# Weight conversions with a scale in place of a maximum and a mask, and a later product for the global tokens

## The chip, the cores and the metric

The kernel runs on one core of a Trainium2 chip. The metric is the time of one execution in microseconds (us) on the device, as the median of several runs. The engines are TensorE (PE in the profile, its weight loads PEld), VectorE (DVE), ScalarE (ACT), GpSimd (POOL) and SyncE (SP), which issues nearly all DMAs. Each engine works through its own queue in order. The profile gives the clock that TensorE is granted as a share of 2.4 GHz; there are two levels, 1.2 and 2.4 GHz.

## What is computed

Three layers in a row. The weights of the second and third layer arrive as 64-bit floats; the rest is 32-bit.

```python
# 1: attention, 4 batches x 8 heads, 512 local tokens (window of 32 to each side) and 32 global tokens, head size 64
a_l = sm([q_l k_g^T, where(mask, q_l k_l^T, -1e9)] / 8);  out_l = a_l @ [v_g, v_l]
out_g = sm(q_g [k_g, k_l]^T / 8) @ [v_g, v_l]
x = out.transpose(0, 2, 1, 3).reshape(2176, 512)      # 2048 local and 128 global tokens
# 2: gated layer, 512 -> 1536 -> 512
gate = 1 / (1 + exp(-(x @ w_gate)));  val = x @ w_val
x = (gate * val) @ w_out
# 3: rational layer, 512 -> 2048 -> 512
h = x @ w_in
P = a0 + a1*h + a2*h**2 + a3*h**3
Q = 1 + |b0|*|h| + |b1|*h**2
out = (P / (Q + 1e-6)) @ w_out
```

## The kernel before

**Number format.** Every operand of a matmul in layers 2 and 3 is split into a high part, rounded to the matmul's format, and a low part, the rest. A product is three matmuls: high by high, high by low, low by high. So each weight must be converted from 64 bits to 32, then split. `Weights` does that in blocks of 128x512, 68 in all: 24 `gv` (gate and value, two to each of the 12 feature blocks of layer 2), 12 `out` of layer 2, and 16 `in` and 16 `out` of layer 3 (the rational blocks). The steps of one block `j`, in the order of `Weights.order`:

- `fetch`: DMA of 512 KB into one of three `raw` buffers, issued by `bits` of three blocks before.
- `magnitude` (L565, L566): two ScalarE instructions, the absolute value of the upper words read as a 32-bit float into `v`, and the lower words scaled by 2^-29 into `q`.
- `bits` (L573 to L575): three VectorE instructions, a maximum with a tiny constant, a shift with a mask, and the OR with the top two bits of the upper word. Then the next fetch.
- `add` (L582): GpSimd adds `q`.
- `hi` (L604): ScalarE casts the high part. `lo` (L612): GpSimd subtracts it for the low part, and DMAs write the result to memory (`keep`); it is loaded again when the ring of twelve weight places has room.
- For the `gv` blocks of the features from 2 on also `sums` (L629 to L632), which forms the four weight sums of Strassen's scheme from two blocks, with VectorE, GpSimd, VectorE, VectorE in a row, and `splits` (L641, L642), two casts and two subtractions.

**Stages.** The attention runs first, to about 125 us, by a list of steps with due times (`STEPS`), into which the first conversions are woven. Then `gated` for layer 2: the tokens stand in five tiles, four of 512 and one (`GLOB`, the 128 global tokens). A first loop, called passes 0 to 5 here, runs over pairs of feature blocks `f0`, `f0 + 1` and treats tiles 0 and 1 and the global tile. In a pass TensorE's order is: first product (gate, then value) of `f0` with tile 0; the two halves of the second product for tile 1 of the pass before; first product of `f0 + 1` with tile 0; the global first product (L721 to L723); first product of `f0` with tile 1; the two halves of the second product for tile 0; two transposes of the global tile (`turn`, L788); first product of `f0 + 1` with tile 1; and the global second product (`second_glob`, L796 to L798). Behind each first product ScalarE takes the sigmoid (L750), VectorE multiplies (L751), ScalarE casts the high part (L758) and VectorE subtracts for the low part (L763). The sums of the second products are added on VectorE (L844, L805 for the global tile).

Between these stands `spot`, which lets `Pace` issue as many of the conversion steps of this pass as its share of 34 us allows; what is left is issued at the end of the pass. So the place of each conversion step in the queues of ScalarE, VectorE and GpSimd is fixed by the program's order. `AT_ONCE` says how many rational blocks are converted in each pass beside the six of the gated layer (pass 5: rational ones alone).

Then tiles 2 and 3: the first two feature blocks plainly, the other ten with Strassen's scheme (`strassen`), seven products in place of eight, with the rest of the conversions spread by another `Pace` over 132 us. From about 585 us on `rational` runs layer 3.

**PSUM.** First products take their banks in turn from a pool of three (`ps1`), second products, `turn` and `second_glob` from a pool of five (`ps2`). A pass takes nine banks of the first pool: two for each of four first products and one for the global one.

Of the kernel before, what the change touches and what calls it, by code (L numbers as in the profile page):

```python
# [8 lines left out]
F32 = mybir.dt.float32  # L9
F32R = mybir.dt.float32r  # L10
U32 = mybir.dt.uint32
AF = mybir.ActivationFunctionType
ALU = mybir.AluOpType
# [11 lines left out]
DM, FF, FF2 = 512, 1536, 2048  # L25
NTOK = B * (S + SG)
BIG = -8.0e9
F64_TINY = 2.0**-15
G1, G2 = 2, 4
Q_CONST = 1.0 + 1e-6  # L30
LN_SCALE = 2.0**-32
# [418 lines left out]
class Weights:  # L450
# [4 lines left out]


    EARLY, AHEAD = 4, 3
    AT_ONCE = (0, 2, 2, 2, 2, 5)
    RING2 = (4, 5, 6, 7, 0, 1, 2, 3, 8, 9, 10, 11)

    def __init__(self, tc, early, dram, ins, outs):
# [14 lines left out]
        for p, f in enumerate(range(2, NF + 1, 2)):  # L476
            m = n + self.AT_ONCE[p]
            if f < NF:
# [76 lines left out]
    def magnitude(self, j):  # L555

        key = self.order[j]
        name = "".join(map(str, key))
        r = self.staged[j]
        if self.combined(key):  # L560
            v = self.only.tile([128, 512], U32, tag="z", name=f"v{name}", bufs=5)
        else:
            v = self.early.tile([128, 512], U32, tag="v", name=f"v{name}", bufs=3)
        q = self.early.tile([128, 512], U32, tag="q", name=f"q{name}", bufs=3)
        self.nc.scalar.activation(v.bitcast(F32), r[:, :, 1].bitcast(F32), AF.Abs)  # L565
        self.nc.scalar.activation(q, r[:, :, 0], AF.Copy, scale=2.0**-29)  # L566
        self.staged[j] = r[:, :, 1], v, q

    def bits(self, j):

        high, v, q = self.staged[j]
        nc = self.nc
        nc.vector.tensor_scalar_max(v.bitcast(F32), v.bitcast(F32), F64_TINY)  # L573
        nc.vector.tensor_scalar(v, v, 3, 0x3FFFFFF8, ALU.logical_shift_left, ALU.bitwise_and)
        nc.vector.scalar_tensor_tensor(v, high, 0xC0000000, v, ALU.bitwise_and, ALU.bitwise_or)  # L575
        if j >= self.EARLY:
            self.fetch(j + self.AHEAD)

# [45 lines left out]
    def sums(self, j):  # L624

        nc, f = self.nc, self.order[j][1]
        v0, v1 = (self.whole[1, f, "gv", k] for k in range(2))
        g0, a0, g1, a1 = v0[:, 0:256], v0[:, 256:512], v1[:, 0:256], v1[:, 256:512]
        nc.vector.tensor_tensor(a1, a0, a1, ALU.add)  # L629
        nc.gpsimd.tensor_tensor(a0, g0, a0, ALU.subtract)  # L630
        nc.vector.tensor_tensor(g0, a1, g0, ALU.subtract)
        nc.vector.tensor_tensor(g1, g1, g0, ALU.subtract)  # L632

# [74 lines left out]
def layer(nc, ps, wp, net, f, i, mh, ml):  # L708

    for k in range(4):  # L710
        wh, wl = wp.block(net, f, i, k)
        nc.tensor.matmul(ps, wh, mh[:, k], start=k == 0, stop=False)  # L712
        nc.tensor.matmul(ps, wh, ml[:, k], start=False, stop=False)  # L713
        nc.tensor.matmul(ps, wl, mh[:, k], start=False, stop=k == 3)  # L714
# [20 lines left out]
def gated(nc, pools, only, xpool, dram, wp, ident, xh, xl):  # L735
# [7 lines left out]
    def new_acc(i):  # L743
        n = TILES[i][1]
        acc[i] = pools.acc.tile([128, 4, n], F32, tag=f"acc{i if i == GLOB else i % 2}", name=f"gacc{i}")

    def gate(pg, pv, name):

        t = pools.t.tile([128, 512], F32, tag="u", name=f"t{name}")[:, 0 : pg.shape[1]]
        nc.scalar.activation(t, pg, AF.Sigmoid)  # L750
        nc.vector.tensor_tensor(t, pv, t, ALU.mult)  # L751
        return t
# [12 lines left out]
    def split(t, name):  # L765
        g = high(t, name)
        low(t, g)
        return g

    def first(f, i):  # L770
        pg = pools.ps1.tile([128, 512], F32, tag="p1", name=f"pg{f}_{i}")
        pv = pools.ps1.tile([128, 512], F32, tag="p1", name=f"pv{f}_{i}")
        layer(nc, pg, wp, 1, f, "gate", xh[i], xl[i])
        layer(nc, pv, wp, 1, f, "val", xh[i], xl[i])
        return split(gate(pg, pv, f"{f}_{i}"), f"{f}_{i}")
# [8 lines left out]
    def turn(f0, t):  # L784

        ps = pools.ps2.tile([128, 512], F32, tag="p2", name=f"pt{f0}")
        for g in range(G):
            nc.tensor.transpose(ps[:, g * 128 : g * 128 + 128], t[:, g * 128 : g * 128 + 128], ident)  # L788
        gh, gl = split(ps[:, 0 : G * 128], f"{f0}_glob")
        return [(gh[:, g * 128 : g * 128 + 128], gl[:, g * 128 : g * 128 + 128]) for g in range(G)]  # L790

    def second_glob(f0, gs):
        ps = pools.ps2.tile([128, 512], F32, tag="p2", name=f"p2{f0}_glob")
        for k, (gh, gl) in enumerate(gs):
            wh, wl = wp.outer(1, f0 + k)
            nc.tensor.matmul(ps, gh, wh, start=k == 0, stop=False)  # L796
            nc.tensor.matmul(ps, gh, wl, start=False, stop=False)
            nc.tensor.matmul(ps, gl, wh, start=False, stop=k == G - 1)  # L798
        if f0 == 0:
            new_acc(GLOB)  # L800
        a = acc[GLOB].rearrange("p m t -> p (m t)")
        if f0 == 0:
            nc.vector.tensor_copy(a, ps)
        else:
            nc.vector.tensor_tensor(a, ps, a, ALU.add)  # L805

    def final_glob():

        n = TILES[GLOB][1]
        ps = pools.ps1.tile([128, 512], F32, tag="p1", name="pty")  # L810
        for m in range(4):
            nc.tensor.transpose(ps[:, m * n : m * n + n], acc[GLOB][:, m], ident)
        yh[GLOB] = xpool.tile([128, 4, n], F32R, tag=f"xh{GLOB}", name=f"yh{GLOB}")
        yl[GLOB] = xpool.tile([128, 4, n], F32R, tag=f"xl{GLOB}", name=f"yl{GLOB}")
        src = ps.rearrange("p (m t) -> p m t", m=4)
        nc.scalar.copy(yh[GLOB], src)
        nc.vector.tensor_tensor(yl[GLOB], src, yh[GLOB].bitcast(F32), ALU.subtract)
# [42 lines left out]
    def pair_of(f0, i, gs):  # L860
        return [lambda h=h: second(f0, i, gs, h) for h in range(2)]
# [7 lines left out]
    def ztile(name):  # L869
        return only.tile([128, 512], F32, tag="z", name=name, bufs=5)  # L870
# [11 lines left out]
    def less(dst, x, y, eng):  # L882

        for d, a, b in zip(dst, x, y):
            eng.tensor_tensor(d, a, b, ALU.subtract)
        eng.tensor_tensor(dst[0], dst[0], dst[1], ALU.add)

    def at(rc, k):
        return [t[:, k] for t in part[rc]]

    def c1(k):
        held["a", k], held["b", k] = ztile(f"za{k}"), ztile(f"zb{k}")
        less((held["a", k], held["b", k]), at((0, 1), k), at((0, 0), k), nc.vector)

    def c2(k):
        h, l = at((1, 1), k)
        a, b = held["a", k], held["b", k]
        nc.gpsimd.tensor_tensor(b, h, a, ALU.subtract)
        nc.gpsimd.tensor_tensor(b, b, l, ALU.add)
# [14 lines left out]
    pending = []  # L914
    for p, f0 in enumerate(range(0, NF, G)):
        pace = Pace(wp.plan[p], 34.0)
        extra = {}
        if f0 + G == NF:
            load = lambda: wp.allow(1)
            extra = {0: [load], 1: [load], 2: [lambda: c1(0)], 3: [load], 4: [load, lambda: c2(0)], 5: [load, lambda: c4(0)],  # L920
                     6: [load, lambda: parks.pop(0)()], 7: [lambda: c3(0)] + [lambda: parks.pop(0)()] * 2,
                     8: [lambda: parks.pop(0)()]}
        spots = iter(range(9))

        def spot(dt):
            pace.advance(dt)
            for step in extra.get(next(spots), []):
                step()

        gs = [first(f0, 0)]  # L930
        if p == 0:
            for step, j in wp.urgent[6:]:
                step(j)
        spot(2 * L)
        for half in pending or [lambda: None] * 2:
            half()
            spot(L if pending else 0)
        gs.append(first(f0 + 1, 0))
        pending = pair_of(f0, 0, gs)
        spot(2 * L)  # L940
        t = first_glob(f0)
        spot(3)
        gs = [first(f0, 1)]
        spot(2 * L)
        for half in pending:
            half()
            spot(L)
        gg = turn(f0, t)
        gs.append(first(f0 + 1, 1))
        second_glob(f0, gg)  # L950
        pending = pair_of(f0, 1, gs)
        for g in range(G):
            for h in range(2):
                wp.release((1, f0 + g, "gv", h))
        spot(0)
        pace.finish()
# [3 lines left out]
    actions = list(wp.plan[-1])  # L960
# [96 lines left out]
            parks.pop(0)()  # L1057

    gs = [first(0, 2)]
    final_glob()  # L1060
    put(0, 0, "a", nc.vector)
    put(1, 0, "b", nc.vector)
    wp.allow(1)
# [5 lines left out]
    park()  # L1069
    wp.allow(1)  # L1070
    gs.append(first(1, 2))
    c1(1)
    park()
    c2(1)
    wp.allow(1)
    pending = pair_of(0, 2, gs)
# [14 lines left out]
        for h in range(2):  # L1091
            wp.release((1, f, "gv", h))
    wp.allow(len(wp.loads))
    pace = Pace(actions, 132.0)
    queue, tail = pair_of(0, 3, gs), []
    for f0 in range(G, NF, G):
        sets, per = ([], []), len(queue) // G
# [293 lines left out]
```

## Time and profile before

| what | us |
|---|---|
| median of 3 runs (lowest, highest) | 972.25 (970.39, 972.79) |
| profiled execution, whole | 973.67 |
| its span, first to last instruction | 971.8 |
| TensorE busy (share of the span) | 912.9 (94%) |
| VectorE busy | 765.8 (79%) |
| ScalarE busy | 580.7 (60%) |
| GpSimd busy | 573.1 (59%) |
| the 16 DMA engines, mean busy share of queue 1 | 47.4% |

Busy times of matmuls are modelled ends of pipelined work, so a busy TensorE is not one at its peak. A wait in the profile is idle time of an engine and what ended it, named by the last semaphore to arrive. Instructions overlap with the next one's start, so the distance of two starts is what an instruction costs its queue, a little less than its duration.

### The profile page before, as it was taken

How to read it: one execution, taken by the hardware profiler on the slowest of the kernel's cores; microseconds unless marked ns; L12 is line 12 of the kernel's file. 1: busy time of each engine (PE TensorE's matmuls, PEld its weight loads, DVE VectorE, ACT ScalarE, POOL GpSimd, SP SyncE). 2: the span in 40 equal slices, each digit the busy share in tenths (PEclk: the TensorE clock that was granted, in tenths of full speed). 3: DMA queues.
4: the chain of work that ended last, by engine and by line, in shares of the span. 5: the costliest groups of instructions: out<-in, count | busy, mean ns of one | idle time of the engine just before them, and what ended most of it. 6: DMA issues, size and time to landing. Idle time of an engine off the chain costs nothing.

```text
span 971.8 us, 13780 instructions
## 1 busy us (share of the span) xinstructions
PE 912.9 (94%) x4666; PEld 752.1 (77%) x4666; DVE 765.8 (79%) x1355; ACT 580.7 (60%) x1161; POOL 573.1 (59%) x470
## 2 busy tenths in 40 slices
PE   8989999869696969799999999999999999999998
PEld 6778888658585858688788887878888888888886
DVE  6988867767777778577777777988788889888887
ACT  6978963435353533424444427777777777777773
POOL 4766764665655555445656665644465667566564
PEclk9999999879797979899999999999999999999999
DMA  9764274766666667659889883202200220020112
GB/s 298 234 202 143 77 250 147 232 207 204 205 212 207 213 206 249 224 201 320 313 315 330 296 323 124 74 1 87 87 1 1 96 77 1 1 87 1 44 54 87
DMA packets 60805, 156.24 MB, mean 161 GB/s; under 512 B 7104, under 2 KB 9152, under 8 KB 60736
## 3 DMA queue, kind: packets, MB, share of 16 engines
q1 hardware_dynamic: 60640, 155.24, 47.4%
q8 instruction: 37, 0.61, 0.2%
q14 instruction: 32, 0.26, 0.1%
q10 hardware_dynamic: 96, 0.13, 0.1%
HBM read 103.17 MB, written 52.17 MB: 160 GB/s over the span
## 4 chain that ended last, share of the span: by engine, by line
PE 73%; DVE 13%; POOL 4%; DMA 4%; issue 3%; ACT 2%; SPq 1%; POOLq 0%; ACTq 0%; DVEq 0%
PE rp L1239 5%; PE rp L1240 5%; PE rp L1241 5%; PE rp L714 5%; PE rp L713 5%; PE rp L712 5%; PE p L832 3%; PE p L830 3%; PE p L831 3%; PE pair L261 2%; PE pg L712 2%; PE pg L713 2%; PE pg L714 2%; PE pv L714 2%; PE pv L712 2%
## 5 line engine op out<-in xcount | busy, mean ns | idle before, releaser
L1156 POOL TENSOR_TENSOR v<-v,u 128x512 f32<-128x512 f32 x68 | 91.3, 1342 | 108.4 <-ACT v L1152 108.2
L1210 POOL TENSOR_TENSOR rgl<-t,rgh 128x512 fp32r<-128x512 f32 x64 | 90.6, 1415 | 40.8 <-issue 18.7
L295 POOL TENSOR_TENSOR p<-p,r 128x448 f32<-128x448 f32 x64 | 58.6, 940 | 37.3 <-DVE r L290 24.8
L1164 DVE TENSOR_TENSOR t<-rp,t 128x512 f32<-128x512 f32 x68 | 46.7, 687 | 41.0 <-ACT t L1160 39.8
L1149 ACT ACTIVATE u<-rp 128x512 f32<-128x512 f32 x68 | 40.4, 595 | 62.1 <-PE rp L714 59.2
L1189 DVE SCALAR_TENSOR_TENSOR t<-t,co,v 128x512 f32<-128x512 f32 x68 | 74.7, 1099 | 2.4
L1185 DVE SCALAR_TENSOR_TENSOR v<-v,u 128x512 f32<-128x512 f32 x68 | 74.2, 1091 | 0.0
L280 ACT ACTIVATE p<-p,mx 128x224 f32<-128x224 f32 x128 | 60.2, 479 | 8.2 <-DVE mx L272 8.2
L844 DVE TENSOR_TENSOR gacc<-p,gacc 128x512 f32<-128x512 f32 x80 | 51.9, 683 | 16.0 <-PE p L832 15.9
L758 ACT CAST gh<-t 128x512 fp32r<-128x512 f32 x38 | 23.5, 619 | 62.2 <-DVE t L751 60.7
L1181 DVE SCALAR_TENSOR_TENSOR v<-v,u 128x512 f32<-128x512 f32 x68 | 58.3, 857 | 1.1 <-ACT u L1177 1.1
L1152 ACT ACTIVATE v<-u,co 128x512 f32<-128x512 f32 x68 | 55.6, 817 | 2.3
L1160 ACT ACTIVATE t<-rp,co 128x512 f32<-128x512 f32 x68 | 51.8, 762 | 2.6 <-POOL rgl L1210 2.6
L1173 ACT ACTIVATE u<-v,co 128x512 f32<-128x512 f32 x68 | 49.2, 724 | 6.2 <-POOL v L1156 6.0
L1168 DVE SCALAR_TENSOR_TENSOR t<-t,co,rp 128x512 f32<-128x512 f32 x68 | 50.2, 738 | 0.0
L1177 ACT ACTIVATE u<-u,co 128x512 f32<-128x512 f32 x68 | 48.5, 713 | 2.3 <-DVE t L1164 2.2
L1198 ACT CAST rgh<-t 128x512 fp32r<-128x512 f32 x64 | 39.1, 611 | 17.8 <-DVE t L1189 17.8
L763 DVE TENSOR_TENSOR gl<-t,gh 128x512 fp32r<-128x512 f32 x38 | 32.3, 849 | 20.8 <-ACT gh L758 20.8
L272 DVE CUSTOM_DVE_ANT_0 p<-pair,masks 128x224 f32<-128x224 f32 x128 | 42.1, 384 | 7.6 <-PE pair L261 5.5
L751 DVE TENSOR_TENSOR t<-pv,t 128x512 f32<-128x512 f32 x28 | 19.2, 685 | 31.7 <-PE pv L714 25.8
L1264 POOL TENSOR_TENSOR racc<-ev,racc 128x512 f32<-128x512 f32 x22 | 37.9, 1743 | 0.0
L261 PE MATMUL pair<-kn,qn 64*128 64x224 f32 x256 | 30.5, 371 | 2.2 <-ACT pgn L319 1.2
(1388 smaller groups left out, 3221.7 us busy)
## 6 DMA issues: line engine op xcount, KB each, us to landing
raw1gv<-in_w_gate_val SPq DMA_DIRECT2D x24, 512.0 KB, 4.2
raw2in<-in_w_in SPq DMA_DIRECT2D x16, 512.0 KB, 4.9
raw2out<-in_w_out SPq DMA_DIRECT2D x16, 512.0 KB, 4.2
kn<-in_k_l SPq DMA_DIRECT2D x15, 448.0 KB, 5.7
raw1out<-in_w_out SPq DMA_DIRECT2D x12, 512.0 KB, 4.0
vn<-in_v_l SPq DMA_DIRECT2D x16, 256.0 KB, 4.0
out<-racc SPq DMA_DIRECT2D x16, 256.0 KB, 2.0
qn<-in_q_l SPq DMA_DIRECT2D x15, 256.0 KB, 5.0
```

The source lines that it names most:

```text
L280: nc.scalar.activation(p, p, AF.Exp, bias=s["mx", half][:, n : n + 1], scale=-1.0, accum_out=s["sm", half][:, n, 0:1])
L295: nc.gpsimd.tensor_tensor(p, p, r, ALU.mult)
L712: nc.tensor.matmul(ps, wh, mh[:, k], start=k == 0, stop=False)
L713: nc.tensor.matmul(ps, wh, ml[:, k], start=False, stop=False)
L714: nc.tensor.matmul(ps, wl, mh[:, k], start=False, stop=k == 3)
L844: nc.vector.tensor_tensor(a, ps[m], a, ALU.add)
L1152: nc.scalar.activation(new(u, "v"), st[u]["u"], AF.Identity, bias=b0, scale=b1)
L1156: nc.gpsimd.tensor_tensor(s["v"], s["v"], s["u"], ALU.mult)
L1181: nc.vector.scalar_tensor_tensor(s["v"], s["v"], Q_CONST, s["u"], ALU.add, ALU.mult)
L1185: nc.vector.scalar_tensor_tensor(s["v"], s["v"], 2.0, s["u"], ALU.subtract, ALU.mult)
L1189: nc.vector.scalar_tensor_tensor(s["t1"], s["t1"], a0, s["v"], ALU.add, ALU.mult)
L1210: nc.gpsimd.tensor_tensor(s["gl"], s["t1"], s["gh"].bitcast(F32), ALU.subtract)
```

## The change

Five things change. `magnitude` gives the absolute value a scale of 2^-112, which shifts the exponent of the upper word to that of a 32-bit float, so `bits` does without the maximum, the shift without the mask, and the OR takes the sign bit alone. In `sums` the one subtraction on GpSimd goes to VectorE. The rational blocks of passes 1 to 4 become one each in place of two, that of pass 5 six in place of five (ten in place of thirteen), and the rest of the conversions, 22 in place of 19, are paced over 146 in place of 132 us. `second_glob` is issued one pass later, behind the first product of `f0` with tile 0 and ahead of the halves for tile 1 of the pass before; that of the last pass is issued where `final_glob` stood, and `final_glob` goes behind the next first product.

```diff
-    AT_ONCE = (0, 2, 2, 2, 2, 5)
+    AT_ONCE = (0, 1, 1, 1, 1, 6)
@@ magnitude
-        self.nc.scalar.activation(v.bitcast(F32), r[:, :, 1].bitcast(F32), AF.Abs)
+        self.nc.scalar.activation(v.bitcast(F32), r[:, :, 1].bitcast(F32), AF.Abs, scale=2.0**-112)
@@ bits
-        nc.vector.tensor_scalar_max(v.bitcast(F32), v.bitcast(F32), F64_TINY)
-        nc.vector.tensor_scalar(v, v, 3, 0x3FFFFFF8, ALU.logical_shift_left, ALU.bitwise_and)
-        nc.vector.scalar_tensor_tensor(v, high, 0xC0000000, v, ALU.bitwise_and, ALU.bitwise_or)
+        nc.vector.tensor_single_scalar(v, v, 3, ALU.logical_shift_left)
+        nc.vector.scalar_tensor_tensor(v, high, 0x80000000, v, ALU.bitwise_and, ALU.bitwise_or)
@@ sums
-        nc.gpsimd.tensor_tensor(a0, g0, a0, ALU.subtract)
+        nc.vector.tensor_tensor(a0, g0, a0, ALU.subtract)
@@ gated, a pass
         spot(2 * L)
+        if pending:
+            second_glob(*last_glob)
         for half in pending or [lambda: None] * 2:
...
-        gg = turn(f0, t)
+        last_glob = f0, turn(f0, t)
         gs.append(first(f0 + 1, 1))
-        second_glob(f0, gg)
@@ gated, behind the passes
     gs = [first(0, 2)]
-    final_glob()
+    second_glob(*last_glob)
...
     gs.append(first(1, 2))
+    final_glob()
...
-    pace = Pace(actions, 132.0)
+    pace = Pace(actions, 146.0)
```

## Rows read from the trace of the kernel before

**Rows 1.** Windows: stretch, length, busy us (instructions) of PE, PEld, DVE, ACT, POOL; clock; DMA.

```profile
206.64:255.22 48.58, 40.41 (x176) 32.85 (x176) 35.30 (x49) 21.20 (x39) 27.72 (x23) 0.89 0.64 206
...
303.44:351.45 48.01, 39.84 (x176) 32.46 (x176) 35.30 (x49) 21.18 (x39) 27.73 (x23) 0.89 0.66 209
351.45:398.05 46.60, 39.75 (x176) 32.35 (x176) 31.39 (x43) 17.78 (x33) 24.18 (x20) 0.90 0.71 246
...
550.00:600.00 50.00, 49.94 (x221) 41.04 (x220) 33.48 (x51) 24.39 (x41) 27.72 (x22) 1.00 0.69 248
```

**Rows 2.** TensorE's waits, whole span: us in total, times, longest us.

```profile
PE p_glob L796 <- ACT gh_glob L758: 32.6, 5, 6.9
PE p_glob L798 <- DVE gl_glob L763: 5.0, 4, 1.3
PE pair L304 <- DMA qgn<-in_q_g: 4.3, 1, 4.3
PE pg L712 <- ACT t L750: 3.9, 1, 3.9
```

**Rows 3.** Time line of TensorE, passes 1 to 5: start, us, line, instruction, wait before it.

```profile
180.88 0.80 PE L712 MATMUL pg<-xh,w12gv 128*128 128x512 f32 x1 [3.88 <-ACT t L750]
...
206.64 0.80 PE L796 MATMUL p_glob<-w12out,gh_glob 128*128 128x512 f32 x1 [6.22 <-ACT gh_glob L758]
...
209.10 0.79 PE L798 MATMUL p_glob<-w12out,gl_glob 128*128 128x512 f32 x1 [1.25 <-DVE gl_glob L763]
...
212.68 0.63 PE L713 MATMUL pg<-xl,w14gv 128*128 128x512 f32 x1
213.11 0.63 PE L714 MATMUL pg<-xh,w14gv 128*128 128x512 f32 x1
...
398.05 0.80 PE L796 MATMUL p_glob<-w110out,gh_glob 128*128 128x512 f32 x1 [5.59 <-ACT gh_glob L758]
```

**Rows 4.** Time line of ScalarE, end of pass 2.

```profile
206.48 0.60 ACT L750 ACTIVATE t<-pg 128x512 f32<-128x512 f32 x1
...
249.09 0.66 ACT L565 ACTIVATE v16out<-raw1out 128x512 f32<-128x512 f32 x1
249.66 0.66 ACT L566 ACTIVATE q16out<-raw1out 128x512 uint32<-128x512 uint32 x1
254.28 0.62 ACT L604 CAST st20in<-v20in 128x512 fp32r<-128x512 f32 x1 [3.97 <-POOL v20in L582]
254.81 0.36 ACT L758 CAST gh_glob<-pt 128x256 fp32r<-128x256 f32 x1
255.07 0.60 ACT L750 ACTIVATE t<-pg 128x512 f32<-128x512 f32 x1
```

**Rows 5.** Time line of VectorE, the same pass.

```profile
239.35 0.43 DVE L574 TENSOR_SCALAR v17gv<-v17gv 128x512 uint32<-128x512 uint32 x1
239.81 0.69 DVE L575 SCALAR_TENSOR_TENSOR v17gv<-raw1gv,v17gv 128x512 uint32<-128x512 uint32 x1
...
241.80 0.69 DVE L763 TENSOR_TENSOR gl<-t,gh 128x512 fp32r<-128x512 f32 x1 [0.69 <-ACT gh L758]
...
247.08 1.28 DVE L844 TENSOR_TENSOR gacc<-p,gacc 128x512 f32<-128x512 f32 x2
...
248.86 1.38 DVE L574 TENSOR_SCALAR v20in<-v20in 128x512 uint32<-128x512 uint32 x1
...
253.03 1.50 DVE L629 TENSOR_TENSOR v17gv<-v17gv,v17gv 128x256 f32<-128x256 f32 x1
...
256.88 0.42 DVE L632 TENSOR_TENSOR v17gv<-v17gv,v17gv 128x256 f32<-128x256 f32 x1
```

**Rows 6.** Time line of GpSimd, the same pass.

```profile
252.99 1.26 POOL L582 TENSOR_TENSOR v20in<-v20in,q20in 128x512 uint32<-128x512 uint32 x1
254.61 0.72 POOL L630 TENSOR_TENSOR v17gv<-v17gv 128x256 f32<-128x256 f32 x1 [0.36 <-DVE v17gv L629]
```

**Rows 7.** Windows of line 573 alone (the maximum): length, DVE busy, instructions.

```profile
206.60:255.20 48.60, 4.82 (x8) 0.89 0.64 206
```

More of the change, by code (lines that the diff above doesn't have):

```diff
@@ L27 @@
 BIG = -8.0e9
-F64_TINY = 2.0**-15
 G1, G2 = 2, 4
```

## The prediction

> **What bounds the kernel now.** I read the windows first, to see in which stretch TensorE has something to win, then TensorE's waits, then the time line of the one stretch that remains, engine by engine. TensorE carries the path: in the stretch 550 to 600 us it is busy 49.94 of 50 us [rows 1], and nothing an edit does to other engines can shorten such a stretch. Pass one is different: each of its passes of 46.6 to 48.6 us has TensorE at 40 us busy and at a granted clock of 0.89 [rows 1]. TensorE's waits say why: 32.6 us in five waits of the global product for the high part cast by ScalarE, 5.0 us for its low part, 3.9 us once for a PSUM bank [rows 2]. A wait costs twice. After it the matmuls start 0.43 us apart [rows 3] where 221 in 50 us are 0.227 us apart [rows 1]: the granted clock is at 1.2 instead of 2.4 GHz. Between the wait that ends at 206.64 and the last such row at 213.11 there are 12 of them, 12 x 0.2 = 2.4 us; behind the later waits I count 8 to 11, 1.6 to 2.2 us. So one pass loses 6.9 + 1.25 + about 2.2 us, some 10.3 us of 48.3 (the mean of the three passes of which rows 1 shows the first and the last); without that it would take about 37.5 us: matmuls and transposes alone are 150 x 0.227 us and 24 of half the width, 37 us. The wait at 180.88 costs 3.9 + 2.6 = 6.5 us (13 matmuls at the low clock), the one at 398.05 costs 5.6 + 1.6 = 7.2 us [rows 3]. All of it together is 6.5 + 4 x 10.3 + 7.2 = 55 us: that is the most the change can take from pass one.
>
> Why is the high part late? ScalarE casts it at 254.81, right behind the high cast of a rational weight at 254.28, which waited 3.97 us for GpSimd's add [rows 4]; that add starts at 252.99 [rows 6], behind a low part and two splits. The next sigmoid stands directly behind, at 255.07 [rows 4]. So the cycle of a pass is not TensorE's but the ring VectorE (bits), GpSimd (add), ScalarE (high cast), GpSimd (low part), in queues that run in order, and I measure it from sigmoid to sigmoid: 206.48 to 255.07, 48.6 us [rows 4].
>
> **The change, part by part.** *The later global product.* It moves one pass border: behind the next first product of tile 0, whose 24 matmuls take 24 x 0.227 = 5.4 us. But the next value product needs the PSUM bank that the sigmoid at 255.07 frees (three banks, nine uses a pass, so the bank comes round exactly), and it starts 12 matmuls = 2.7 us behind the border. So TensorE will no longer wait for the high and low part; it waits for that sigmoid, if the sigmoid is late by more than 2.7 us. With ScalarE's queue unchanged this alone would turn 6.9 + 1.25 us into 6.9 + 0.9 - 2.7 = 5.1 us, some 3 us a pass. The step that moves issues six matmuls and one VectorE instruction (0.6 us, as others over 512 columns) and no DMA; that instruction now stands ahead of two accumulations of tile 1, where only the two banks they free wait for it. The outer weights it reads are released later still, behind the second product, so no load on SP's queue moves. The conversion of the global result for the next layer (four transposes, one cast, one subtraction) goes behind one more first product; its reader comes 200 us later: nothing.
>
> *One conversion fewer in each of passes 1 to 4* (7 in place of 8): two ScalarE instructions of 0.66 us and a cast of 0.62 us [rows 4], two VectorE instructions that stay, 0.43 and 0.69 us [rows 5], two of GpSimd of 1.26 us [rows 6], one fetch and one write of 512 KB on SP's queue, which then has less ahead of the stage writes. Pass 5 has six in place of five.
>
> *The maximum and the mask.* The maximum goes: eight instructions cost 4.82 us in one pass [rows 7], 0.6 us each, some because GpSimd held them up. The shift without its mask and the OR stay as they are (0.43 and 0.69 us undisturbed). ScalarE's Abs with a scale is the same instruction form over the same 512 columns: 0.66 us, as now. The instruction beside it, which scales already, takes 0.66 us too [rows 4], so I take 0, and 0.1 us either way as bounds.
>
> *The subtraction of the sums on VectorE.* GpSimd's 0.72 us [rows 6] goes, and with it two hand-overs. VectorE's four instructions of 128x256 take 0.42 us each, 0.36 us start to start, when GpSimd rests, and 1.50 us when it is working [rows 5]. I take one such wait for a set of four, 2.7 us in all, because GpSimd has one ready instruction at that place and then waits for a cast. The bounds are 1.5 us (none) and 6.0 us (each of the four).
>
> *The new cycle, walked from sigmoid to sigmoid* in the order of the queues that the code gives (the prices are those of [rows 4 to 6]): sigmoid, product, cast and low part of tile 1 2.75 us; bits of an outer weight 1.05 (3.8); the sums 2.7 (6.5); product, cast, low part of tile 0 2.0 (8.5); bits with one wait for GpSimd 2.3 (10.8); global evacuation 0.6 (11.4); two accumulations 1.2 (12.6); bits, met by the splits on GpSimd, 3.1 (15.7); low part and add on GpSimd 2.5 (18.2); cast and sigmoid 1.25 (19.45); product, cast, low part 2.05 (21.5); bits 1.05 (22.5); add, cast, low part, add 5.0 (27.5); cast and magnitude 1.7 (29.2); sigmoid to low part 2.7 (31.9); bits 1.0 (32.9); sums 2.7 (35.6); two accumulations 1.2 (36.8); bits 1.2 (38.0); add, cast, magnitude, global cast 3.3: 41.3 us. TensorE's own 37.5 us lies inside it. Without any wait between VectorE and GpSimd it is 35.5 us, so TensorE would set the end; with a wait at every place where both have ready work it is 45 us or more. I take 41.3: what remains for TensorE is a wait of about 2 to 4 us a pass for the bank.
>
> *Sum*, against the profiled execution (span 971.8 us, 973.67 us with what lies around it, 1.42 us above the median of 972.25). Passes 2 to 4: 3 x (48.3 - 41.3) = 21.0 us. Pass 1: the wait at 180.88 goes, since tile 0's sigmoid now stands ahead of the cast that waits for GpSimd, 6.5 us, and 2.2 us of its end: 8.7 us (it carries one more set of splits than the others). Pass 5, 46.6 us [rows 1], has one conversion more, and the casts of finished sums wait there for stage buffers until their DMAs have landed; the same walk gives 43.0 us, bounds 40 and 47: 3.6 us. Behind it the first product no longer waits in line behind the global one: from the sigmoid to its end stood 30 matmuls, 8 of them at the low clock, 8.4 us; now 18, 13 of them at the low clock, 6.7 us: 1.7 us. Attention: the wait of 4.3 us for a small query load [rows 2] stands on SP behind a fetch that waits for bits of a weight; a maximum less there, 0.7 us. Against it: the conversions in the second half are 22 in place of 19 and now reach to its end. Their tail (three conversions: 3 x 1.1 us VectorE, 3 x 1.9 us ScalarE, 3 x 2.6 us GpSimd) lies beside idle time: in 550 to 600 VectorE works 33.48, ScalarE 24.39 and GpSimd 27.72 us of 50 [rows 1]. So nothing, and 3 us if that cover is gone, since the rational units behind start on the same queues; I take 1.0 us. 21.0 + 8.7 + 3.6 + 1.7 + 0.7 - 1.0 = 34.7 us: 971.8 - 34.7 = 937.1 us of span, and 972.25 - 34.7 = 937.5 us for the median.
>
> One rule speaks against the change. The rows show a 0.42 us instruction of VectorE at 1.50 us while GpSimd works [rows 5]. The Trainium skill, "SBUF — State Buffer", section "SBUF: two separate sides", says that VectorE and GpSimd take turns at one pair of ports, held for a whole instruction, and that a VectorE instruction with two SBUF inputs is among those that are shut out. By it the change turns a GpSimd subtraction into a fourth VectorE instruction that GpSimd can block. With every one of them blocked the two sets of sums in the cycle would take 12.0 us in place of 5.4, the cycle 47.9 us, and the kernel about 963 us.
>
> **Rivals.** *A, TensorE alone sets the passes.* The queues overlap better than I walked them, the cycle falls under 37.5 us. For it: 35.5 us without waits between VectorE and GpSimd. Against it: every bits step met by GpSimd now shows a wait. The 6.5 + 4 x 10.3 us of passes 1 to 4 and 6 of pass 5 go: 972.25 - 54 = 918 us. *B, the wait only moves.* VectorE gives back at GpSimd's locks what the maximum freed: L574 took 1.38 us behind GpSimd [rows 5], and whatever stands first there pays that. The cycle stays at 45 to 47 us, at 46 us 3 x 2.3 + 6.5 + 2.4 (pass 5 and attention) = 16 us are won: 956 us. *C, slower.* The second half, where TensorE now has no slack, gets three more conversions, and their DMAs share SP's one queue with the weights of the ten Strassen products. If a fetch arrives late, ScalarE stands at a magnitude and the sigmoid behind it is late; each such stop costs what the one at 180.88 costs, 6.5 us [rows 3]. From six of ten products on the gain is gone; all ten give 972.25 - 35 + 65 = 1002 us. Against it: TensorE is busy to 49.94 of 50 there, and ScalarE idles half the time. *D, the change does not reach the path*: the sigmoid is late by other work, 970 to 974 us; the 3 us of the moved product alone speak against it.
>
> **How the numbers follow.** The forecast (cycle 39 to 44 us, 926 to 948) has 0.57, A 0.16, B 0.19, C 0.05, D 0.03. The range goes from A's 918 to 958, which holds B's price; about 0.15 lie outside. A measurement of this kernel tells about 0.3% from no change. Faster by more than that: 0.57 + 0.16 + 0.19 = 0.92; within it 0.03; slower 0.05.
>
> **What would show it.** In TensorE's waits the 32.6 and 5.0 us for the global product should be gone or under 3 us, and a wait of the value product of tile 0 for the sigmoid of tile 1 stand in their place, 2 to 4 us in each of passes 1 to 4 and longer (3 to 6 us) at the end of pass 5. Sigmoid to sigmoid should be 41 us. VectorE should have 68 instructions fewer from the maximum and ten more of 128x256, GpSimd ten fewer. The wait at 180.88 should be gone. From 600 us on the trace should be the same, shifted. The prediction is wrong if the passes run at 37.5 us (A), if a wait of 5 us or more stays at each border (B), or if TensorE shows waits between 370 and 560 us (C).

## The result and the profile after

The changed kernel takes 942.66 us (median of four runs, 940.72 to 944.15), the kernel before, on the same chip, 972.52 (970.39 to 972.98). The ratio is 0.9696, with a 95% interval of 0.9669 to 0.9723: 29.9 us less where the prediction had 34.7. The profiled execution took 940.72 us with a span of 938.9, 32.9 us less than the span before, so the sum below is made against 32.9. It was the quickest of its four, 1.9 us under their median, while that of before was 1.4 us over its own: with these 3.3 us taken off, the profiles tell 29.6, as the medians do.

The page's row of busy times of the changed kernel:

```profile
PE 901.1 (96%) x4666; PEld 745.8 (79%) x4666; DVE 730.4 (78%) x1297; ACT 580.2 (62%) x1161; POOL 566.6 (60%) x460
```

VectorE lost 58 instructions, 68 maxima less ten subtractions that came, and 35.4 us; GpSimd lost the ten. TensorE lost 11.8 us of busy time with the same matmuls.

Windows of the changed kernel, with the columns of rows 1. They run from sigmoid to sigmoid for passes 2 to 5; then come the stretch to the first Strassen product, the Strassen stage, and the stretch up to the first transposes of the rational layer:

```profile
196.47:238.70 42.23, 39.31 (x176) 32.47 (x176) 29.76 (x41) 20.42 (x39) 25.00 (x20) 0.94 0.68 219
...
280.24:321.71 41.47, 37.73 (x176) 31.18 (x176) 29.01 (x41) 19.29 (x37) 23.89 (x19) 1.00 0.66 214
321.71:368.20 46.49, 37.48 (x176) 31.13 (x176) 31.36 (x41) 16.96 (x32) 27.86 (x22) 0.96 0.79 272
368.20:402.10 33.90, 33.24 (x143) 27.40 (x143) 26.58 (x32) 13.57 (x25) 16.43 (x12) 0.95 0.59 204
402.10:546.60 144.50, 144.50 (x638) 119.22 (x636) 102.70 (x145) 66.03 (x116) 92.70 (x73) 1.00 0.93 334
546.60:611.10 64.50, 60.59 (x266) 49.21 (x264) 54.19 (x69) 48.55 (x77) 41.65 (x29) 1.00 0.30 108
```

The last four stretches of the kernel before, cut at the same places of the program:

```profile
351.30:397.90 46.60, 39.75 (x176) 32.35 (x176) 31.37 (x42) 17.78 (x33) 24.18 (x20) 0.90 0.71 245
397.90:434.29 36.39, 36.24 (x154) 29.87 (x155) 26.05 (x33) 12.41 (x23) 16.55 (x12) 0.95 0.52 178
434.29:581.02 146.73, 145.91 (x638) 118.88 (x636) 109.77 (x160) 60.88 (x108) 90.09 (x70) 1.00 0.89 317
581.02:643.71 62.69, 60.59 (x265) 49.22 (x263) 54.00 (x67) 47.81 (x76) 37.76 (x26) 1.00 0.26 88
```

Read stretch by stretch, the 32.9 us come together like this:

| stretch | before, us | after, us | won | forecast |
|---|---|---|---|---|
| attention, to pass 0's first product | 125.78 | 121.63 | 4.15 | 0.7 |
| pass 0 | 28.05 | 28.04 | 0.0 | 0 |
| pass 1 | 52.65 | 46.80 | 5.85 | 8.7 |
| passes 2 to 4 | 144.82 | 125.24 | 19.6 | 21.0 |
| pass 5 | 46.60 | 46.49 | 0.1 | 3.6 |
| to the first Strassen product | 36.39 | 33.90 | 2.5 | 1.7 |
| Strassen stage | 146.73 | 144.50 | 2.2 | 0 |
| to the rational layer's transposes | 62.69 | 64.50 | -1.8 | -1.0 |
| the rest | 328.1 | 327.8 | 0.3 | 0 |

TensorE's waits in the changed kernel, in the form of rows 2:

```profile
PE pv L710 <- ACT t L748: 21.8, 5, 9.0
PE pair L303 <- DMA qgn<-in_q_g: 3.6, 2, 3.3
PE rp L1239 <- DVE gacc L842: 2.9, 1, 2.9
```

The 32.6 and 5.0 us for the global product [rows 2] are gone, and so is the 3.9 us wait at 180.88 [rows 3]. In their place TensorE waits five times at a value product for the sigmoid of tile 1. TensorE's time line shows where (start, us, instruction, wait before it):

```profile
197.13 0.79 PE L710 MATMUL pv<-xh,w14gv 128*128 128x512 f32 x1 [4.93 <-ACT t L748]
...
239.35 0.79 PE L710 MATMUL pv<-xh,w16gv 128*128 128x512 f32 x1 [2.92 <-ACT t L748]
...
322.36 0.50 PE L710 MATMUL pv<-xh,w110gv 128*128 128x512 f32 x1 [3.68 <-ACT t L748]
...
368.86 0.80 PE L710 MATMUL pv<-xh,w10gv 128*128 128x512 f32 x1 [9.02 <-ACT t L748]
```

That is the new wait that the prediction named. At the ends of passes 1 to 4 it takes 4.93, 2.92, 1.23 and 3.68 us (the third, at 280.89, is not in the fence), 3.2 us in the mean; forecast were 2 to 4. At the end of pass 5 it takes 9.02 where 3 to 6 were forecast.

### The profile page after: what moved, and what is told of

It is laid out like the page before. It is cut to its first block, busy times and chain, and to the rows that moved or that the text cites. A ratio compares the mean times of both kernels' runs of the same rounds, so it can differ in the third digit from the quotient of the medians.

```text
span 938.9 us, 13719 instructions
## 1 busy us (share of the span) xinstructions
PE 901.1 (96%) x4666; PEld 745.8 (79%) x4666; DVE 730.4 (78%) x1297; ACT 580.2 (62%) x1161; POOL 566.6 (60%) x460
## 4 chain that ended last, share of the span: by engine, by line
PE 63%; DVE 11%; POOL 9%; issue 7%; DMA 4%; ACT 4%; SPq 1%; POOLq 0%; ACTq 0%; DVEq 0%
PE rp L1239 6%; PE rp L1241 6%; PE rp L1240 6%; PE rp L712 5%; PE rp L710 5%; PE rp L711 5%; PE p L829 2%; PE p L828 2%; PE p L830 2%; PE pair L260 2%; DVE t L1189 1%; PE bank L361 1%; PE bank L379 1%; PE pv L710 1%; PE bank L363 1%
## 5 line engine op out<-in xcount | busy, mean ns | idle before, releaser
L1164 DVE TENSOR_TENSOR t<-rp,t 128x512 f32<-128x512 f32 x68 | 46.8, 688 | 41.2 <-ACT t L1160 40.0
L271 DVE CUSTOM_DVE_ANT_0 p<-pair,masks 128x224 f32<-128x224 f32 x128 | 42.2, 384 | 7.5 <-PE pair L260 5.6
```

## What makes the sigmoid late now

ScalarE, end of pass 3 of the changed kernel, which answers to rows 4:

```profile
278.34 0.62 ACT L602 CAST st20in<-v20in 128x512 fp32r<-128x512 f32 x1 [3.01 <-POOL v20in L580]
278.87 0.67 ACT L564 ACTIVATE v19out<-raw1out 128x512 f32<-128x512 f32 x1
279.44 0.65 ACT L565 ACTIVATE q19out<-raw1out 128x512 uint32<-128x512 uint32 x1
279.99 0.35 ACT L756 CAST gh_glob<-pt 128x256 fp32r<-128x256 f32 x1
280.24 0.60 ACT L748 ACTIVATE t<-pg 128x512 f32<-128x512 f32 x1
```

VectorE, the same place, which answers to rows 5:

```profile
270.80 0.42 DVE L627 TENSOR_TENSOR v18gv<-v18gv,v18gv 128x256 f32<-128x256 f32 x1
271.25 1.39 DVE L628 TENSOR_TENSOR v18gv<-v18gv 128x256 f32<-128x256 f32 x1
272.67 0.42 DVE L629 TENSOR_TENSOR v18gv<-v18gv,v18gv 128x256 f32<-128x256 f32 x1
273.13 1.54 DVE L630 TENSOR_TENSOR v18gv<-v18gv,v18gv 128x256 f32<-128x256 f32 x1
274.59 1.28 DVE L842 TENSOR_TENSOR gacc<-p,gacc 128x512 f32<-128x512 f32 x2
275.79 0.41 DVE L572 TENSOR_SCALAR v20in<-v20in 128x512 uint32<-128x512 uint32 x1
276.24 0.69 DVE L573 SCALAR_TENSOR_TENSOR v20in<-raw2in,v20in 128x512 uint32<-128x512 uint32 x1
276.85 1.28 DVE L842 TENSOR_TENSOR gacc<-p,gacc 128x512 f32<-128x512 f32 x2
```

GpSimd, the same place, which answers to rows 6:

```profile
270.96 1.40 POOL L580 TENSOR_TENSOR v19gv<-v19gv,q19gv 128x512 uint32<-128x512 uint32 x1 [3.47 <-DVE v19gv L573]
273.08 1.30 POOL L610 TENSOR_TENSOR w19gv<-v19gv,w19gv 128x512 fp32r<-128x512 f32 x1 [0.73 <-ACT w19gv L602]
277.01 1.30 POOL L580 TENSOR_TENSOR v20in<-v20in,q20in 128x512 uint32<-128x512 uint32 x1 [2.62 <-DVE v20in L573]
```

The ring of the prediction is still there. The sigmoid at 280.24 stands behind a high cast that waited 3.01 us for GpSimd's add; that add waited 2.62 us for VectorE's bits of the same block; the bits stood behind the weight sums and two accumulations, in which VectorE never rests. Two of the four sums, L628 and L630, ran while GpSimd was inside an instruction and took 1.39 and 1.54 in place of 0.42 us. This set costs 274.59 - 270.80 = 3.8 us, the other set of the pass, at 242.38, 2.7. The Trainium skill, "SBUF — State Buffer", section "SBUF: two separate sides", speaks of an exclusive lock between VectorE and GpSimd, held for whole instructions: the trace agrees with the lock. The 12.0 us that the prediction worked out for it, with every VectorE instruction of two sets blocked, did not come: the two sets together take 6.5.

## Experiments: each part alone, and each part taken back

Four kernels add one part to the kernel before, four take one part out of the changed kernel.

**The scale.** The edit, added in `one_scale`, taken back in `less_scale`:

```diff
-        self.nc.scalar.activation(v.bitcast(F32), r[:, :, 1].bitcast(F32), AF.Abs)
+        self.nc.scalar.activation(v.bitcast(F32), r[:, :, 1].bitcast(F32), AF.Abs, scale=2.0**-112)
-        nc.vector.tensor_scalar_max(v.bitcast(F32), v.bitcast(F32), F64_TINY)
```

(and the shift and the OR that go with it).

> The kernel before with the scale in place of maximum and mask alone. Theory: eight maxima fewer in a pass, 4.8 us of VectorE of which most lies on the ring: passes of 44 to 45 us in place of 48.3, and some of the 3.6 us that the attention won; 950 to 956 us. Rival (the ports: whatever stands first behind GpSimd pays its wait): passes of 47 us or more, 963 to 970 us.

Measured: 957.37 us, ratio 0.9842 (0.9821 to 0.9864). The cycles of passes 2 to 4 fell from 48.6, 48.2 and 48.0 to 45.5, 46.6 and 45.6 us, the attention ended 2.05 us earlier, and the Strassen stage took 144.48 us. The time lies between the two expectations, 1.4 us above the theory's, and so do the cycles.

> The changed kernel with maximum and mask back. Theory: seven instructions of 0.42 to 1.5 us a pass, most of them on the ring: passes of 44 to 46 us, the attention's 3.6 us lost too; 957 to 965 us. Rival (ports): 945 to 950 us.

Measured: 961.66 us, ratio 0.9891 (0.9874 to 0.9908). The cycles are 45.0, 44.3 and 44.3 us, the attention ends at 125.3, the Strassen stage takes 146.84 us. So the scale is worth 15 us alone and 19 us within the whole, the largest part of the change. The rival, that locks between VectorE and GpSimd give back what the maximum freed, falls. In `one_scale`, `less_later`, `less_sums` and `less_ten` the Strassen stage takes 144.5 us, in `one_later`, `one_ten`, `one_sums` and `less_scale` 146.6 to 147.5: its 2.2 us belong to the scale.

**The later product.** The edit, added in `one_later`, taken back in `less_later` (with it `final_glob` moves, as in the change):

```diff
+        if pending:
+            second_glob(*last_glob)
         for half in pending or [lambda: None] * 2:
...
-        second_glob(f0, gg)
```

> The kernel before with the later global product alone. Theory (the ring of VectorE, GpSimd and ScalarE sets a pass): the ring is as long as before, TensorE only waits elsewhere, for the bank that the sigmoid frees, some 5 us a border in place of 8.2; 2 to 4 us a pass are won, about 958 us. Rival (the place of the product is the gain): nearly all of it, 943 to 946 us, waits under 3 us.

Measured: 960.78 us, ratio 0.988 (0.9862 to 0.9898). TensorE's waits in `one_later`:

```profile
PE pv L712 <- ACT t L750: 26.1, 5, 5.8
PE pg L712 <- ACT t L750: 4.4, 2, 3.9
```

> The changed kernel with the global product at its old place. Theory: with the short ring the product's wait for the low part puts TensorE's next first product behind the ring, so the ring itself grows: passes of 44 to 46 us in place of 41.7, 953 to 960 us. Rival (the ring alone counts, the place nothing): 943 to 946 us.

Measured: 955.96 us, ratio 0.983 (0.9813 to 0.9847); the wait for the cast of the global product is back, 31.4 us in five times. The moved product is worth 12 us alone, 13 us within the whole. Alone it leaves bank waits of 4.3 to 5.8 us, where the prediction's step had 5.1, and cycles of 45.7 us, 2.6 less than before, where it had "some 3 us a pass". The wait at 180 stays (3.9 us): it was not this part that removed it. The time is 2.8 us above the 958 expected.

**The sums on one engine.** The edit, added in `one_sums`, taken back in `less_sums`:

```diff
-        nc.gpsimd.tensor_tensor(a0, g0, a0, ALU.subtract)
+        nc.vector.tensor_tensor(a0, g0, a0, ALU.subtract)
```

> The kernel before with the sums on VectorE alone. Theory: each set saves the hand-over to GpSimd and back (0.85 us wait, 0.72 us GpSimd) and pays one wait for GpSimd: 1 to 2 us a pass, 963 to 968 us. Rival (by the rule of the shared ports VectorE's four instructions each wait for GpSimd): no gain or a loss, 972 to 985 us.

Measured: 971.88 us, ratio 0.9988 (0.9976 to 1.0001): no change that this measurement can tell. Cycles of 47.4 to 47.7 us are 0.3 to 1.2 less than before. The theory's 963 to 968 us are missed; the rival's "no gain" came, but not its lock on all four: VectorE's set at 249.14 takes 1.51, 0.42, 1.51 and 0.42 us.

> The changed kernel with one subtraction of the sums back on GpSimd. Theory: 1 to 2 us a pass lost, 947 to 952 us. Rival (ports): the four instructions on VectorE are each held by GpSimd, so it is faster with GpSimd, 938 to 942 us.

Measured: 946.11 us, ratio 0.973 (0.9712 to 0.9749). Its cycles are 0.7 to 0.8 us longer than the changed kernel's. The time is just under the theory's range, and its interval overlaps that of the changed kernel (0.9669 to 0.9723). So this part is worth 3.5 us by the medians here and nothing that can be told alone; it is small, as the lock on two of four sums lets one expect.

**Ten conversions in place of thirteen.** The edit, added in `one_ten`, taken back in `less_ten`:

```diff
-    AT_ONCE = (0, 2, 2, 2, 2, 5)
+    AT_ONCE = (0, 1, 1, 1, 1, 6)
...
-    pace = Pace(actions, 132.0)
+    pace = Pace(actions, 146.0)
```

> The kernel before with ten rational conversions in pass one and the slower pace alone. Theory: one conversion of eight less on the ring, 4 to 5 us in each of passes 1 to 4, nothing or a loss of 1 to 3 us in pass 5 with its six; 955 to 960 us. Rival (the sums and the splits hold the ring, not the number of conversions): under 1.5 us a pass, 967 us or more.

Measured: 976.34 us, ratio 1.0035 (1.0019 to 1.0051): slower than before. The theory's gain did not come; the rival's expectation, under 1.5 us a pass and 967 us or more, holds, though neither named a loss. TensorE's waits in `one_ten`:

```profile
PE p_glob L796 <- ACT gh_glob L758: 43.9, 5, 12.0
...
PE rp L1239 <- DVE gacc L844: 3.3, 1, 3.3
```

Passes 2 to 4 gain only 0.3 to 1.3 us each, pass 5 grows from 46.6 to 52.3, and the stretch ahead of the rational transposes from 62.7 to 65.0.

> The changed kernel with thirteen rational conversions in pass one and the old pace. Theory: passes 1 to 4 at 45 to 46 us, pass 5 and the start of the third layer a little shorter: 953 to 958 us. Rival (the number of conversions is hidden): within 2 us of 942.7 us, or under it.

Measured: **934.93 us**, ratio 0.9621 (0.9599 to 0.9643), whose interval lies below that of the changed kernel: taking this part back makes the kernel faster by 7.7 us. That is what the rival expected; the prediction's step is wrong. Against the changed kernel pass 1 is longer (49.4 for 46.8) and passes 2 to 4 are the same (42.2, 41.2 and 41.2 for 42.2, 41.5 and 41.5), but pass 5 takes 40.9 for 46.5, the stretch behind it 32.5 for 33.9, and the stretch to the transposes 62.7 for 64.5 us.

## Experiments: where the ten conversions cost

**Pass 5.** ScalarE at the end of pass 5 of the changed kernel:

```profile
360.40 0.62 ACT L602 CAST st23out<-v23out 128x512 fp32r<-128x512 f32 x1 [4.18 <-POOL v23out L580]
366.21 0.62 ACT L845 CAST sty<-gacc 128x512 fp32r<-128x512 f32 x1 [5.19 <-DMA k90y<-sty]
367.42 0.62 ACT L845 CAST sty<-gacc 128x512 fp32r<-128x512 f32 x1 [0.59 <-DMA k22out<-st22out]
367.94 0.37 ACT L756 CAST gh_glob<-pt 128x256 fp32r<-128x256 f32 x1
368.20 0.60 ACT L748 ACTIVATE t<-pg 128x512 f32<-128x512 f32 x1
```

Two casts of finished sums (`park`) wait 5.19 and 0.59 us until earlier results have left the three stage buffers, and the global cast and the sigmoid for which TensorE waits 9.02 us stand behind them. In `less_ten` the same two casts wait less:

```profile
361.78 0.62 ACT L845 CAST sty<-gacc 128x512 fp32r<-128x512 f32 x1 [2.33 <-DMA k24in<-st24in]
364.30 0.62 ACT L845 CAST sty<-gacc 128x512 fp32r<-128x512 f32 x1 [1.90 <-DMA k90y<-sty]
```

The run `park` issues these casts later in the changed kernel:

```diff
-                     6: [load, lambda: parks.pop(0)()], 7: [lambda: c3(0)] + [lambda: parks.pop(0)()] * 2,
-                     8: [lambda: parks.pop(0)()]}
+                     6: [load], 7: [lambda: c3(0)],
+                     8: [lambda: parks.pop(0)()] * 4}
```

> The changed kernel, with the four steps that put finished sums of pass 5 away issued later: all behind the second first product of tile 1, in place of beside its two pair products. Theory (stage buffers): the 9.0 us that TensorE waits at the end of pass 5 come from ScalarE standing 5.19 and 0.59 us at casts of finished sums, whose stage buffers still wait for the DMAs of earlier results; the global cast and the sigmoid stand behind them. Issued later, the casts no longer stand ahead of the sigmoid: pass 5 takes 40 to 42 us in place of 46.5, the kernel 936 to 939 us. Rival (the six conversions of pass 5 fill the ring): pass 5 stays at 45 to 47 us, the kernel at 941 to 945 us.

Measured: 938.89 us, ratio 0.9654 (0.9632 to 0.9676). Windows of `park`, pass 5 and the stretch behind it, and its ScalarE at the end of the pass:

```profile
322.90:360.34 37.44, 36.79 (x174) 30.91 (x175) 30.90 (x40) 15.24 (x29) 23.38 (x18) 1.00 0.85 285
360.34:400.17 39.83, 35.44 (x146) 28.35 (x145) 27.71 (x35) 15.20 (x28) 20.88 (x16) 0.91 0.65 226
```

```profile
360.08 0.36 ACT L756 CAST gh_glob<-pt 128x256 fp32r<-128x256 f32 x1
360.34 0.60 ACT L748 ACTIVATE t<-pg 128x512 f32<-128x512 f32 x1
```

Pass 5 falls from 46.5 to 37.4 us, below what was expected, and TensorE's wait at its end is gone, with six conversions still in the pass: the casts that stood for stage buffers ahead of the sigmoid were its cause. But of the 9.1 us the kernel keeps 3.1 to the first Strassen product, since the stretch behind grows from 33.9 to 39.8 us: the casts stand there now, and TensorE waits 4.4 us for a sigmoid at 381.23. By the medians 3.8 us remain, and the intervals of the two kernels touch (0.9676 and 0.9669).

`five` leaves one conversion out of pass 5:

```diff
-    AT_ONCE = (0, 1, 1, 1, 1, 6)
+    AT_ONCE = (0, 1, 1, 1, 1, 5)
```

> The changed kernel with five conversions in pass 5 in place of six (nine in pass one, 23 in the second half). Theory 1 (the sixth conversion costs: its cast and its DMA stand ahead of the sums'): pass 5 takes about 41 us as with the thirteen conversions, the kernel 936 to 939 us. Theory 2 (which conversions stand in pass 5, and so which DMAs are under way there, decides): pass 5 stays at 45 to 47 us, the kernel 941 to 945 us. With 23 in the second half the first rational product may wait 3 us or more.

Measured: 940.01 us, ratio 0.9663 (0.9646 to 0.968). Pass 5 takes 44.2 us, between the two expectations: the sixth conversion explains 2.3 of the 5.6 us between 46.5 and 40.9. The other 3.3 us lie between two kernels with five conversions in pass 5 each; in `five` the casts of sums there wait 2.90 and 1.88 us for DMAs, about as in `less_ten`, but the ones of the weights ahead of them stand at other places. Which of these steps makes the 3.3 us stays open.

**The tail.** In `less_ten` and in the kernel before, the first rational product that needs a sum of the Strassen stage waits 1.1 us for VectorE's last accumulation (L1239); in every kernel with 22 or 23 conversions in the second half and its pace of 146 us it waits 2.9 to 3.6, and the stretch to the transposes takes 64.5 to 65.3 in place of 62.7 us. In the changed kernel the last conversions reach to the end of the Strassen stage (546.60). There GpSimd still has an add of one of them ahead of its gate product (`t`), for which ScalarE's cast and then VectorE's low part wait:

```profile
547.84 1.28 POOL L580 TENSOR_TENSOR v215out<-v215out,q215out 128x512 uint32<-128x512 uint32 x1
549.08 1.28 POOL L1037 TENSOR_TENSOR t<-s,t 128x512 f32<-128x512 f32 x1
```

```profile
550.40 0.62 ACT L756 CAST gh<-t 128x512 fp32r<-128x512 f32 x1 [1.81 <-POOL t L1037]
```

```profile
551.05 1.11 DVE L761 TENSOR_TENSOR gl<-t,gh 128x512 fp32r<-128x512 f32 x1 [3.13 <-ACT gh L756]
```

VectorE's low part starts 4.5 us behind the end of the stage, and VectorE is idle for 3.13 us before it. In `less_ten`, where GpSimd is done with the last conversion 3.6 us before the end of the stage (542.13), it starts 2.2 us behind. That this delay is what made the wait at L1239 1.8 us longer is the likely reading; no run tests it. The number and the pace were not varied apart.

`best` moves one conversion from pass 1 into the second half, against `less_ten`:

```diff
-    AT_ONCE = (0, 2, 2, 2, 2, 5)
+    AT_ONCE = (0, 1, 2, 2, 2, 5)
```

> The changed kernel with (0,1,2,2,2,5) conversions in its six passes, twelve in all, in place of (0,1,1,1,1,6), and the second half's conversions spread over 132 us again. Pass 1 took 46.8 us with one conversion and 49.4 with two, pass 5 46.5 with six and 40.9 with five. Theory 1 (the number in a pass decides): pass 1 about 47, passes 2 to 4 about 41.5, pass 5 about 41: 931 to 934 us, some 2 us below the version with (0,2,2,2,2,5). Theory 2 (the place of each conversion in the order decides): pass 5 is back at 44 to 47 us, 936 to 942 us.

Measured: 936.23 us (932.52 to 938.41), ratio 0.9631 (0.9609 to 0.9653). In its profile pass 1 takes 46.8, pass 2 43.6, passes 3 and 4 41.2, pass 5 40.8 us, and the wait at L1239 is 1.1 us with 20 conversions in the second half. Passes 1 and 3 to 5 are what the first theory expects; pass 2 is some 2 us longer, and the median is 2.2 us above its range and in that of the second, whose 44 to 47 us for pass 5 did not come. By the medians it can't be told from `less_ten`. Both are faster than the kernel before and the changed one.

**Ring or bank.** `bank4` gives the first products a fourth bank, taken from the second products:

```diff
-        self.ps1 = ctx.enter_context(tc.tile_pool(name="ps1", bufs=3, space=PSUM))
-        self.ps2 = ctx.enter_context(tc.tile_pool(name="ps2", bufs=5, space=PSUM))
+        self.ps1 = ctx.enter_context(tc.tile_pool(name="ps1", bufs=4, space=PSUM))
+        self.ps2 = ctx.enter_context(tc.tile_pool(name="ps2", bufs=4, space=PSUM))
```

> The changed kernel with four PSUM banks for the value products and four for the rest, in place of three and five. Theory (the ring of VectorE, GpSimd and ScalarE sets the passes): one bank more lets TensorE run ahead once and is then used up; passes 2 to 4 stay at 41 to 42 us, the kernel at 938 to 944 us. Rival (the bank itself sets them): the wait for the sigmoid goes, passes 2 to 4 take 37 to 39 us, the kernel 925 to 932 us.

Measured: 958.39 us, ratio 0.9857 (0.9831 to 0.9884), outside both. TensorE's waits in `bank4`:

```profile
PE pt L786 <- DVE gacc L842: 18.5, 5, 5.6
PE p L828 <- DVE gacc L801: 6.5, 1, 6.5
```

The wait for the sigmoid is gone, and the transposes of the global tile wait for VectorE's accumulations to free one of the four other banks; passes 2 to 4 take 43.8 to 44.0 us. So the second products lose by giving up the fifth bank. What a fourth bank without this price would give is not shown by it, so how much of the remaining 3 us a pass is the bank's stays open.

## Why the prediction was right, and where it was not

**What bounds the kernel.** Right for the kernel before: the waits at pass borders were the ring's, and with VectorE relieved and the global product moved the passes fell from 48.3 to 41.7 us in the mean of passes 2 to 4 (125.24 / 3); the walk gave 41.3. That it came so close is in part luck: by the same reasoning the passes of `less_ten`, with one conversion more, were expected at 45 to 46 us, and passes 2 to 4 there took 41.2 to 42.2. So the ring has room for a conversion that the walk, which lays its steps end to end, doesn't see. Rival A needed 37.5 and is out (48.3 less the 10.3 us lost would be 38.0; that slip changes nothing), B needed 45 to 47 and is out, and so is D. C needed waits in the Strassen stage; that stage has TensorE busy for 144.50 of 144.50 us at a DMA share of 0.93, so three more conversions are hidden there until its end.

The prediction put the Strassen stage at nothing, since no edit to other engines shortens a stretch like 550 to 600 us [rows 1]. But the whole stage of the kernel before had TensorE busy for 145.91 of 146.73 us, with small stops at the products `pb`, the longest of them for a sum of VectorE:

```profile
476.59 0.50 PE L976 MATMUL pb<-txh,w15g 128*128 128x512 f32 x1 [0.65 <-DVE s L991]
```

In the changed kernel these stops are gone, all but one near the start of the stage, and with them 2.2 us.

**The later product.** Right in mechanism and size: the new wait is at the named instruction, and alone it comes near to what the step worked out.

**The maximum.** Right that the scale costs ScalarE nothing: 0.67 us at 278.87 for the scaled absolute value, 0.66 before [rows 4]. The term for the attention was mis-sized: 0.7 us forecast, 4.15 measured. The wait for the query load fell only from 4.3 to 3.6 us; other waits there went too (one for VectorE at 8.49, 0.7 us, and one for ScalarE at 24.95, 1.2 us, have no counterpart that long), and the mean granted clock of the stretch rose from 0.97 to 1.00. Most of it is the scale's: 2.05 us alone, 3.7 us when taken back. The sizes are rough: the attention ends between 124.4 and 125.8 us in the five profiles without the scale and between 120.8 and 123.7 in the nine with it.

**The sums.** One lock for a set was taken, 2.7 us; the two sets take 2.7 and 3.8 us. The term of 5.4 us is 6.5, inside its bounds.

**One conversion fewer.** This is the step that failed. It counted seven conversions in place of eight as a gain in passes 1 to 4. In the new ring passes 2 to 4 don't notice the number (41.5 us with one rational block, 41.2 with two), so that the walk's cycle came out right with a term that is worth nothing there; pass 1 alone wins 2.6 us by it. What the step cost as a whole is in `less_ten`: without it the kernel is 7.7 us faster. What the moved conversions cost lay in other terms: pass 5, 3.6 us forecast and 0.1 won, since the prediction named the waits for stage buffers and didn't price them, and the tail, 1.0 forecast and 1.8 lost. Set against the table, the terms that were too high (pass 1 by 2.8, passes 2 to 4 by 1.4, pass 5 by 3.5, the tail by 0.8) make 8.5 us, those that were too low (attention 3.4, Strassen 2.2, the stretch ahead of it 0.8, the rest 0.3) 6.7: the sum missed the span by only 1.8 us because they nearly cancel. That is luck.

**Pass 1.** 8.7 us forecast, 5.85 won. The wait at 180.88 went as said, and it was the second rational block of the pass that made it: it is gone in every profile with one such block in pass 1 and stands, at 2.2 to 3.9 us, in every one with two. But at the border behind it 4.93 us remain, the longest of the first four.

## What to carry to other kernels

Where three engines hand work round in queues that run in order, walk the ring from one landmark to its next return: it named the wait and gave the new cycle within 1 us here, though it overpriced a conversion by some 4 us, since it lays steps end to end that can overlap. Work taken from an engine that others in the ring wait for (the maximum) pays at every return. Work that is moved out of a ring is paid for where it lands: price the buffers and the DMAs of the stage that takes it, above all at a border where an engine's queue ends in a cast for a buffer that is not yet free. A part of a change is judged by taking it out of the whole: of the four here the scale and the later product gain 19 and 13 us, the sums 3.5 by medians whose intervals overlap, the fourth costs 8, and the sum alone hid it.

## What the runs showed of the hardware

Behind waits of 2.9 to 3.7 us, TensorE's clock doesn't follow the length of the wait. Windows of 5 us behind three of them, two of the changed kernel behind 3.68 and 2.92 us, and one of `five` behind 3.63 us:

```profile
322.30:327.30 5.00, 4.94 (x22) 4.09 (x23) 4.17 (x7) 1.12 (x3) 2.59 (x2) 1.00 0.85 311
239.30:244.30 5.00, 4.95 (x12) 3.88 (x13) 4.18 (x7) 1.12 (x3) 2.57 (x2) 0.50 0.86 285
```

```profile
321.40:326.40 5.00, 4.92 (x12) 3.86 (x13) 4.16 (x7) 1.14 (x3) 2.58 (x2) 0.50 0.90 298
```

Behind 3.68 us the granted clock was 1.00 and 22 matmuls fitted into the window, behind 2.92 us it was 0.50 with 12. The third window is the same border as the first, since `five` is the same program up to pass 5: nearly the same wait, and the clock at 0.50. The prediction's 1.6 to 2.6 us at the low clock were counted behind waits of 3.9 to 6.9 us and don't carry over to waits as short as these; a wait cut from 5 to 3 us may or may not give them back. The Trainium skill, "TensorE: Matmul & The Clock Gate", section "Part 1: The HAM clock gate", says that the point at which the clock changes varies from run to run of one kernel; the first and the third window agree.
